# Attention and a fast-matrix-product SwiGLU block on one core: fewer and larger transfers, reciprocals between two transposes, one layout for all queries and keys

## The chip, the core and the metric

The kernel runs on one core of one Trainium2 chip. The core has a matrix engine (PE, TensorE) with its weight loader (PEld), a vector engine (DVE), a scalar engine (ACT), a general engine (POOL, GpSimd) and a queue engine (SP) that issues transfers. Each engine takes its instructions strictly in the order in which they were emitted, and a transfer that SP or ACT issues is carried out by 16 DMA engines that all queues share. The metric is the device time of one execution in microseconds (us); lower is better.

## The reference

An attention block with normalised queries and keys feeds a SwiGLU block. Shapes: 8 batches, 12 heads, 448 positions, 64 per head; 3584 tokens of 768, hidden width 1536.

```python
def rmsnorm(x, g):
    rms = np.sqrt(np.mean(x * x, axis=-1, keepdims=True) + 1e-06)
    return x / rms * g
q_n, k_n = (rmsnorm(q, g_q), rmsnorm(k, g_k))
scores = scale * np.matmul(q_n, k_n.transpose(0, 1, 3, 2))
attn = np.exp(scores - np.max(scores, axis=-1, keepdims=True))
attn = attn / (np.sum(attn, axis=-1, keepdims=True) + 1e-09)
attn_out = np.matmul(attn, v)
...
x = attn_out.transpose(0, 2, 1, 3).reshape(B * S, H * D)
g = x @ w_gate
silu = g * (1.0 / (1.0 + np.exp(-g)))
out = silu * (x @ w_val) @ w_out
```

The three weight matrices arrive as 64-bit floats, which the kernel turns into 32-bit floats itself.

## The kernel before

**Staging.** All that runs is in `fast`. Two heads of one batch are a pair; there are 48 pairs, m = 0 to 47, six to a batch. The products with the weights use a scheme that multiplies 3x3 blocks with 15 products over two batches at a time: so there are four blocks of two batches (12 pairs) each. The order on the matrix engine is: attention of pairs 0 to 11 (`EARLY`), then for each block the up products (`up_product`, L1400: 120 units of 4 matmuls, read out by ACT and DVE) and the down products (`down_product`, L1574), and among the down products of a block the attention of the next twelve pairs.

**A pair** (`attention`, from L709) runs: load q and k (`load`, L730 to 737), on SP, and for k of pair 0 on ACT's queue; squares on ACT (L767); sums on DVE (L787 or L793); a swap of partial sums on ACT (L803); a reciprocal root on ACT and DVE (`inverse_root`, L682 to 690); scaling on POOL (L827 or L834); transposition; scores on PE (L912) into one of two PSUM buffers; exponentials on ACT (L927); weighted sums on PE (L988) with the values that L754 and L757 loaded; column sums on PE (L1019); their reciprocal on DVE (`invert`, L1054); for early pairs a product that spreads it (L1062); copy, join and division on ACT and DVE (L1077, L1080, L1084). The queries and keys of a pair take two of four buffers named `qk`; the next loads wait until the query buffer has been read by L868 (`queries`), which for the usual layout stands after DVE's block transposes (L865).

**The first two pairs** (`NATURAL`) are loaded differently: 112 partitions with four consecutive positions each, so that a row of a transfer is 1 KB; PE transposes them with an identity matrix (L853) and ACT and DVE copy the result (L859, L861). With pair 0's second square, PE also issues four products of no use to the result (L770). All other pairs are loaded with rows of 32 numbers (128 bytes), four transfers to a tensor, and DVE transposes blocks of 32 by 32.

**Weights.** 24 conversions (`convert`): 16 for the up side (four to each quarter g of the up products) and 8 for the down side. Each loads 9 blocks of 64-bit values in five transfers (L1208 three, L1210 two) to a place, lets ACT scale (L1218, L1222) and DVE round (L1240, L1246, L1252), lets POOL form 11 sums and differences of blocks (L1271, L1274), and stores 15 blocks in one transfer to a buffer in memory (L1299). `load_sides` (L1360) fetches them again for the products, in pieces of five or two block names. Places: `GT`, `HS`, `ES`, `XS`, `PAIRS`, `SPARE`, which are buffers that other work uses at other times (`PAIRS` is the pairs' `work`, `ES` holds exponentials); a load into `ES`, `PAIRS` or `GT[2]` waits for `last_exp`, the column sums of pair 11. `turns` and `counts` name the places: six conversions run beside the early pairs, eighteen afterwards, and these round by way of a PSUM bank (`by_bank`).

**The order** is not written out by hand. Each step is a piece given to `Order.add` with an engine, an assumed cost, a due time (`when`, lowered by `rank`), the pieces that it follows and the buffers that it takes. `Order.run` plans a time for each piece with those costs, greedily, and emits the pieces in planned order; `LEAD` and `PAIR` set the due times of the early pairs. So a changed cost, due time or transfer count moves instructions past each other on every engine. The plan has no effect at run time other than this order; semaphores do the waiting.

## Time and profile before

| | before |
|---|---|
| median of 3 runs (lowest to highest) | 1484.42 us (1483.13 to 1485.69) |
| the profiled execution: time, span | 1484.42 us, 1482.6 us |
| PE busy | 1435.1 us (97%), 6696 matmul instructions |
| DVE, ACT, POOL busy | 914.8, 680.7, 416.0 us |
| packets moved | 409457, of which 316804 under 512 B; 193.30 MB |

The span is the time from the first to the last recorded instruction; about 1.8 us of the execution's time lie outside it. The page gives busy times per engine, then the span in 40 slices, the transfer queues, a chain of waits followed back from the end, groups of instructions by source line, and transfers. Beside the page the trace can be asked for the instructions of a stretch in order of time: start, duration, engine, line, operation, output and input with shapes, how many were merged, and, in square brackets, how long the engine stood idle before it and what released it. "SPq" and "ACTq" are the issue of transfers. The twelve early pairs take the first 140 us, the first up products 140 to 328 us.

### The profile page before, as it was taken

Reading aid. Unit: us, or ns where it says so; the run is one execution under the profiler, and the core shown is the slowest. Engines: PE = TensorE matmul, PEld = TensorE weight load, DVE = VectorE, ACT = ScalarE, POOL = GpSimd, SP = SyncE. Lnnn points to the kernel's source line nnn. Section 1 sums busy time; section 2 is a strip of 40 time slices with the busy share of each in tenths; the row PEclk is TensorE's granted clock in tenths of the full one; section 3 lists DMA queues with packets and bytes.
Section 4 is the critical chain, followed back from the end, with each engine's and each line's share of the span. In section 5 each row is a group of like instructions: output and inputs, shape, how many; then the busy total and the mean of one; then the engine's idle time right before and its main releaser. Section 6 shows DMA issues by size and latency. Waiting matters only on the chain.

```text
span 1482.6 us, 19482 instructions
## 1 busy us (share of the span) xinstructions
PE 1435.1 (97%) x6696; PEld 680.7 (46%) x6696; DVE 914.8 (62%) x1403; ACT 680.7 (46%) x1358; POOL 416.0 (28%) x470
## 2 busy tenths in 40 slices
PE   6989999999999999999999999999999999999998
PEld 2434554443444455544444445554444445555553
DVE  3878897877978544355886733454786753432533
ACT  5864544437775321445767422354676532122100
POOL 3545585636444100012534200011343410000000
PEclk8999999999999999999999999999999999999999
DMA  6677999974453431533344432352444442222235
GB/s 166 160 162 215 294 331 335 289 213 92 98 117 84 111 107 71 144 98 89 78 110 107 101 118 72 110 132 77 97 101 103 89 123 85 80 98 73 83 98 107
DMA packets 409457, 193.30 MB, mean 130 GB/s; under 512 B 316804, under 2 KB 391428, under 8 KB 403204
## 3 DMA queue, kind: packets, MB, share of 16 engines
q1 hardware_dynamic: 397840, 190.35, 47.8%
q10 hardware_dynamic: 11380, 1.61, 0.7%
q8 instruction: 55, 0.90, 0.3%
q14 instruction: 54, 0.44, 0.1%
q0 software_dynamic: 128, 0.00, 0.0%
HBM read 157.29 MB, written 34.60 MB: 129 GB/s over the span
## 4 chain that ended last, share of the span: by engine, by line
PE 73%; ACT 3%; DVE 3%; issue 1%; DMA 1%; SPq 1%; ACTq 0%; DVEq 0%
PE mm L1574 22%; PE mm L1400 20%; PE at L1400 20%; PE st L912 6%; PE at L988 5%; PE st L1019 1%; ACT spare L1072 1%; ACT es L927 1%; SPq L737 1%; DVE rd L1054 1%; DVE ss L807 0%; DMA work<-in_k_dram 0%; DMA out_dram<-spare 0%; DVE ss L793 0%; ACT ss L803 0%
## 5 line engine op out<-in xcount | busy, mean ns | idle before, releaser
L1400 PE MATMUL at<-xs,ws 128*128 128x448 f32 x960 | 400.6, 540 | 4.3 <-DVE v L1346 3.1
L1400 PE MATMUL mm<-xs,ws 128*128 128x448 f32 x960 | 401.0, 540 | 3.6 <-DVE spare L1348 2.2
L1400 PEld LDWEIGHTS at<-xs,ws 128*128 128x128 f32 x960 | 181.9, 190 | 184.8 <-issue 172.1
L1400 PEld LDWEIGHTS mm<-xs,ws 128*128 128x128 f32 x960 | 181.6, 190 | 184.3 <-issue 172.0
L834 POOL TENSOR_TENSOR work<-work,rr 128x448 f32<-128x448 f32 x92 | 101.8, 1126 | 480.1 <-DVE rr L690 353.3
L1574 PE MATMUL mm<-gt,ws 128*128 128x448 f32 x448 | 177.2, 545 | 0.0
L912 PE MATMUL st<-work 64*64 64x448 f32 (+1 forms) x1536 | 156.4, 514 | 18.0 <-ACT es L927 7.5
L1344 DVE TENSOR_TENSOR gt<-gt,mm 128x448 f32<-128x448 f32 x64 | 39.7, 620 | 184.2 <-PE mm L1400 181.9
L1574 PE MATMUL mm<-hs,ws 128*128 128x448 f32 x384 | 152.1, 545 | 0.9 <-DVE ss L688 0.9
L927 ACT ACTIVATE es<-st 128x896 f32<-128x896 f32 x129 | 114.1, 912 | 54.3 <-PE at L988 42.6
L932 POOL TENSOR_TENSOR sums<-es 128x896 f32<-128x896 f32 x36 | 75.8, 2104 | 196.0 <-PE st L1019 83.4
L1474 ACT ACTIVATE st<-gt 128x448 f32<-128x448 f32 x96 | 52.3, 546 | 168.9 <-DVE gt L1348 90.3
L1072 ACT COPY spare<-rd 32x224 f32<-32x224 f32 x288 | 108.1, 375 | 35.4 <-DVE rd L1054 31.1
L1574 PEld LDWEIGHTS mm<-gt,ws 128*128 128x128 f32 x448 | 82.9, 190 | 84.2 <-issue 80.6
L988 PE MATMUL at<-es,v 64*64 64x448 f32 x1032 | 109.9, 544 | 2.7 <-DVE ss L688 2.5
L1342 ACT COPY gt<-mm 128x448 f32<-128x448 f32 x80 | 42.5, 532 | 140.4 <-PE mm L1400 140.4
L1574 PEld LDWEIGHTS mm<-hs,ws 128*128 128x128 f32 x384 | 71.1, 190 | 72.9 <-issue 70.6
L912 PEld LDWEIGHTS st<-work 64*64 64x64 f32 x1536 | 50.8, 135 | 98.8 <-issue 38.1
L1342 ACT COPY v<-at 128x448 f32<-128x448 f32 x96 | 51.1, 532 | 85.1 <-PE at L1400 81.0
L932 POOL TENSOR_TENSOR sums<-sums,es 128x896 f32<-128x896 f32 x36 | 78.7, 2186 | 2.8
L865 DVE STREAM_TRANSPOSE work<-work 128x448 f32<-128x448 f32 x92 | 56.6, 627 | 25.5 <-POOL work L834 22.8
L988 PEld LDWEIGHTS at<-es,v 64*64 64x64 f32 x1032 | 39.5, 134 | 63.0 <-issue 58.7
(161 smaller groups left out, 1589.1 us busy)
## 6 DMA issues: line engine op xcount, KB each, us to landing
ws<-up_sides SPq DMA_DIRECT2D x32, 1024.0 KB, 5.0
ws<-down_sides SPq DMA_DIRECT2D x16, 1024.0 KB, 5.0
ws<-down_sides SPq DMA_DIRECT2D x28, 512.0 KB, 4.3
ws<-up_sides SPq DMA_DIRECT2D x16, 768.0 KB, 4.4
work<-in_q_dram SPq DMA_DIRECT2D x184, 56.0 KB, 2.4
work<-in_k_dram SPq DMA_DIRECT2D x184, 56.0 KB, 2.4
out_dram<-spare SPq DMA_DIRECT2D x168, 56.0 KB, 1.9
v<-in_v_dram SPq DMA_DIRECT2D x96, 96.0 KB, 2.6
```

What stands on the lines that cost most here:

```text
L834: nc.gpsimd.tensor_tensor(out=tiles["t", m][:, x], in0=tiles["qk", (m, x)], in1=rr.to_broadcast([P, NC, C]), op=ALU.mult,)
L865: nc.vector.transpose(to, tiles["t", m][:, x].rearrange("p c f -> p (c f)"))
L912: nc.tensor.matmul(st[ds(D * x, D), h, 0:n], tiles["KT", m][rows, ds(P * j + D * of_keys, D)], tiles["QT", m][rows, ds(Q * of_queries, n)] ...
L927: nc.scalar.activation(e, tiles["st", (m, j)][:, :, 0 : S * width(j) // P], AF.Exp)
L932: nc.gpsimd.tensor_tensor(out=to, in0=tiles["e", (m, 0)] if j == 1 else to, in1=e, op=ALU.add)
L988: nc.tensor.matmul(tiles["at", (m, x)][ds(D * h, D), queries], tiles["v", m][rows, j, h], tiles["e", (m, j)][rows, h], start=j == 0, stop= ...
L1072: nc.scalar.copy(inv[ds(D * h + C * to, C), ts(x, Q)], tiles["rd", m][ds(D * h + C * x, C)])
L1342: nc.scalar.copy(to, ps)
L1344: nc.vector.tensor_tensor(out=to, in0=old, in1=ps, op=ALU.add)
L1400: nc.tensor.matmul(ps(), w[:, at, which, c], xs[:, SLOT[x], c], start=fresh and c == 0, stop=c == NC2 - 1, skip_group_check=True,)
L1474: nc.scalar.activation(take(*act, [P, 2, TB])[:, 0, 0:S], to, AF.Silu)
L1574: nc.tensor.matmul(banks[s][:, 0:S], w[:, at, s, g], where[x][:, g], start=fresh and g == 0, stop=g == NG - 1, skip_group_check=True,)
```

## The change

1. `NATURAL` and everything that served it are gone: the identity, L770, L853, L859, L861. Pairs 0 and 1 are loaded and transposed like all others. `LEAD` is 14.0 in place of 10.0.
2. `load_six`: for the early pairs the values of three pairs come in one step of five transfers into half of `spare`, in place of four transfers to each pair. There are two such halves, so the third step waits for the weighted sums of pair 2 and the fourth for those of pair 5.
3. `invert`: DVE transposes the sums in blocks of 32 by 32, takes the reciprocal of one column of each block (7 numbers to a partition), and transposes them back with the column repeated.
4. `convert`: raw values lie behind the converted ones; three transfers with three blocks each in place of five; the order of the blocks and of the 15 stored blocks changes with it, so that a fetch by `load_sides` is often one run in place of two.
5. The sixth early conversion uses `GT[0]` for a second time in place of `SPARE`; a load into `SPARE` waits for `last_exp` too; the early conversions have a rank of 30 in place of 0.

```diff
-    EARLY = 2 * NPAIR
-    NATURAL = (0, 1)
-    UP_SUMS = (8, 1, 7, 13, 10, 14, 3, 5, 11, 0, 4)
-    DOWN_SUMS = (1, 10, 14, 3, 11, 0, 4, 5, 8, 7, 13)
-    BLOCKS = (6, 2, 12, 9)
+    UP_SUMS = (10, 14, 3, 8, 1, 7, 13, 5, 11, 0, 4)
+    DOWN_SUMS = (3, 10, 14, 1, 11, 0, 4, 5, 8, 7, 13)
+    BLOCKS = (6, 9, 2, 12)
...
-    LEAD, PAIR = 10.0, 9.0
+    LEAD, PAIR = 14.0, 9.0
...
+        def load_six():
+            x = take("ve", m // 3, None)
+            for j in range(NJ):
+                for p in (0, D) if j == NJ - 1 else (0,):
+                    n = D if j == NJ - 1 else P
+                    rows = v[b][2 * c : 2 * c + 6, ds(P * j, n)].rearrange("h s d -> s h d")
+                    nc.sync.dma_start(x[ds(p, n), j], rows)
...
-            if m == 0 and x:
-                for _ in range(4):
-                    nc.tensor.matmul(banks[0], chosen[0:R, 0], of, start=True, stop=True)
...
         def invert():
-            nc.vector.reciprocal(take("rd", m, [P, Q]), tiles[den])
+            rd, rc = take("rd", m, [P, Q]), take("rc", m, [P, Q // C])
+            nc.vector.transpose(rd, tiles[den])
+            nc.vector.reciprocal(rc, rd.rearrange("p (c i) -> p c i", i=C)[:, :, 0])
+            every = rc.rearrange("p (c one) -> p c one", one=1).to_broadcast([P, Q // C, C])
+            nc.vector.transpose(rd, every)
...
         inv = add(
-            "DVE", 1.52, when + 4.0, invert, after=[all_sums], uses=[] if of_bank else [den],
-            takes=[("rd", m)],
+            "DVE", 0.95, when + 4.0, invert, after=[all_sums], uses=[] if of_bank else [den],
+            takes=[("rd", m), ("rc", m)],
         )
...
-        rank = 20.0 if by_bank else 0.0
+        rank = 20.0 if by_bank else 30.0
...
-        raw, dst = places[place][:, 0 : 2 * VALUES], places[place][:, 2 * VALUES : PLACE]
+        dst, raw = places[place][:, 0:VALUES], places[place][:, VALUES:PLACE]
-        wait = [last_exp[0]] if place in (ES, PAIRS, GT[2]) else []
+        wait = [last_exp[0]] if place in (ES, PAIRS, GT[2], SPARE) else []
...
-            for i, n, rows in ((0, 2, (1, 3, 0)), (2, 2, (0, 2, 2)), (5, 3, (0, 3, 1))):
-                nc.sync.dma_start(to[:, i : i + n], src(slice(*rows[:2]), rows[2]))
-            for i, k, n in ((4, 0, 0), (8, 2, 2)):
-                nc.sync.dma_start(to[:, i], src(k, n))
+            for at, n in ((slice(3, 8, 2), 0), (slice(0, 3), 1), (slice(8, 3, -2), 2)):
+                nc.sync.dma_start(to[:, at], src(slice(0, 3), n))
-            "SP", 2.5, when - 12.0, load, after=[staged.get(place), *wait], kb=1152, early=3.0
+            "SP", 1.6, when - 12.0, load, after=[staged.get(place), *wait], kb=1152, early=3.0
...
-        sides = places[place].rearrange("p (b f) -> p b f", f=P)[:, 7:22]
-        at = {x: i for i, x in enumerate(sums)}
+        sides = places[place].rearrange("p (b f) -> p b f", f=P)[:, 5:20]
+        at = {x: i for i, x in enumerate((*BLOCKS, *sums))}
...
-    turns = [(*XS, *GT[:2], HS, SPARE), (ES, PAIRS, GT[2], SPARE, HS), (ES, PAIRS, HS, SPARE), (ES, HS)]
+    turns = [(*XS, *GT[:2], HS, GT[0]), (ES, PAIRS, GT[2], SPARE, HS), (ES, PAIRS, HS, SPARE), (ES, HS)]
```

The order of the built programs shows what moved. On SP, the sixth raw load of weights stood between the keys of pair 7 and the values of pair 8; it now stands behind the last keys of the early pairs. The third step of values stands before the queries of pair 6, the fourth before those of pair 9. On DVE, the block transposes of pair 11 stand behind the reciprocal of pair 10, and the first conversion by bank that follows the early pairs is a second one in `HS`, ahead of the one in `ES`. On PE, one up product and the spread of pair 10 stand ahead of the weighted sums of pair 11. The first fetch of the second quarter's weights stood behind the raw loads into `ES` and `PAIRS`; it now stands behind the stores from `PAIRS` and from `GT[2]` and the raw load into `PAIRS`.

## The prediction

> **What bounds the kernel now.** First the page's head. PE is busy 97% of the span, so only PE's idle and slow stretches can be won.
>
> ```profile
> PE 1435.1 (97%) x6696; PEld 680.7 (46%) x6696; DVE 914.8 (62%) x1403; ACT 680.7 (46%) x1358; POOL 416.0 (28%) x470
> ...
> PEclk8999999999999999999999999999999999999999
> DMA  6677999974453431533344432352444442222235
> ```
>
> The second and third lines cut the span into 40 slices. Transfers are near full only in slices 5 to 8 (148 to 297 us), where the weights are converted. 1482.6 - 1435.1 = 47 us of idle PE; the busy times by stretch put 23.5 of them before 140 us, 10 into 140 to 420 and 14 into all the 1063 us behind, the last stores among them. So the change is decided in the early pairs and shortly behind them. Next, these stretches (us; then busy time and instructions of PE, PEld, DVE, ACT, POOL, the granted clock, the transfers' share, GB/s):
>
> ```profile
> 60.00:70.00 10.00, 10.00 (x122) 4.46 (x113) 8.58 (x15) 8.76 (x17) 5.54 (x11) 1.00 0.57 99
> 70.00:80.00 10.00, 7.42 (x84) 3.70 (x82) 7.92 (x14) 6.96 (x14) 7.67 (x12) 1.00 1.02 270
> 80.00:90.00 10.00, 6.84 (x82) 3.36 (x82) 6.99 (x9) 6.51 (x10) 3.71 (x6) 0.91 0.74 164
> 90.00:100.00 10.00, 10.00 (x96) 4.04 (x88) 5.35 (x12) 7.11 (x17) 5.68 (x10) 0.75 0.68 158
> 120.00:130.00 10.00, 8.23 (x100) 3.51 (x96) 9.83 (x13) 6.48 (x9) 7.51 (x12) 1.00 0.82 288
> ```
>
> Up to 70 us ACT and DVE pace the pairs together. From 70 to 90 all engines lose, with the transfers full at first; towards the end DVE is full. The column sums (L1019) give the pace: pair 0 ends at 37.6 us, 1 at 45.0, 5 at 82.1, 6 at 97.8, 8 at 113.1, 10 at 133.7, 11 at 139.1. One step, from pair 5 to 6, takes 15.7 us where about 9 are usual. The order in time of SP, ACT and PE says why:
>
> ```profile
> 70.32 3.58 SPq L1208 DMA_DIRECT2D spare<-in_moe_w_gate_dram  x3
> ...
> 77.50 0.55 SPq L1299 DMA_DIRECT2D up_sides<-xs  x1
> 78.37 4.86 SPq L737 DMA_DIRECT2D work<-in_q_dram  x4
> 83.28 2.21 SPq L737 DMA_DIRECT2D work<-in_k_dram  x4
> ...
> 87.86 0.58 ACT L767 ACTIVATE work<-work 128x448 f32<-128x448 f32 x1 [1.84 <-DMA work<-in_k_dram]
> 88.35 0.53 ACT L927 ACTIVATE more<-st 128x448 f32<-128x448 f32 x1
> ...
> 88.92 3.27 PE L912 MATMUL st<-work 64*64 64x448 f32 x16 [3.16 <-ACT more L927]
> ```
>
> The raw load of the sixth conversion and a store stand on SP ahead of pair 8's queries. Their issue takes 4.86 us where 1.9 to 2.0 are usual, the keys land late, ACT waits at their square, the exponentials of pair 7 stand behind that square, and PE idles 3.16 us. It then runs slow: the same 16 matmuls take 3.27 us here, 1.70 at 100.35 us. At 76.22 PE waited 2.48 us more, behind pair 7's late keys.
>
> **The change part by part.** PE needs no more instructions than before; each term says how much earlier or later PE gets through.
>
> *The first two pairs.* Removed: 8 warming matmuls (6.75 us from 6.83 us) and 16 transposes. Added: rows of 128 bytes for 1 KB, four issues of 0.48 us for one of 0.45, so +1.5 us on SP for each of three tensors, and a swap (0.88 us) and four block transposes (0.62 each) in place of two copies a pair. Following the lines in order: SP issues q0, q1, k1 until 0.75 + 3 x 1.95 = 6.6 us; ACT issues k0 by about 3.4; landing takes at most 3.7 us in this trace, so k0 is there by 7.1 and k1 by 10.3. Then square 0.58, sum 1.08, swap 0.88, 0.19, root 0.46, three times 0.2, POOL twice 0.92: 12.7 us. DVE's order puts pair 1's sum first (ready at 10.3 + 0.58 + 1.08, about 12.6 us behind ACT's other steps), then 2 x 0.62 and the queries' 0.67: first scores at 14.6 to 16.5 us. Before they start at 16.45, because PE was busy with the warming products until 12.93 and DVE was held twice. The second pair is then ahead by some 5 us, but ACT has about 3 us less of weight conversion behind it. I take -1 us, from -2 to +3. The rows that bear on the lost warming: at 16.45 and 20.26 us the scores ran at full rate (8 matmuls in 0.98 us), at 28.41 slow again (16 in 3.27). So warming bought a few microseconds at most, and the upper end of +3 holds it.
>
> The Trainium skill, "TensorE: Matmul & The Clock Gate", Part 1, says that an idle array runs at half rate until about 3.4 us of sustained work, which speaks against dropping the warming products; going by it this term would be about 1.7 us worse. "DMA: Bandwidth & Descriptors", Specifications, asks for 512 bytes or more in a transfer's run, which speaks against the new loads of the first pairs; this trace has 316804 of 409457 packets below that already.
>
> *Fewer issues on SP.* Values: a pair's four issues take 0.92 + 1.27 = 2.19 us, twelve pairs 26.3. Three pairs take 3 x 0.46 + 2 x 0.63 = 2.6, four times: 10.6. Raw weights: 1.46 + 0.96 = 2.42 to 1.46, five times before the last pair. About 20 us of SP's early time go, and the sixth raw load leaves the stretch altogether: it stands behind the last keys. With it goes what made pair 8 late. The stretch costs 2.48 + 3.16 us idle and, in the slow matmuls from 88.92 to 95.7 us (3.27 for 1.70, 1.72 for 0.93, 2.42 for 1.68), 3.1 more: 8.7 us. The price of the bundling: the third step of values waits for pair 2's weighted sums and stands before pair 6's loads, the fourth waits for pair 5 and stands before pair 9's. Each adds 2.6 us of issue and some 800 KB at the 270 GB/s of the full stretch, 3 us, ahead of those keys; PE meanwhile has one pair's weighted sums, sums and scores (2.6 + 1.9 + 1.2 + 2.6 us) to do. I take two thirds: -5.8 us; bounds -8.7 and 0.
>
> *Reciprocals.* One took 1.55 us. No row has a block transpose of PSUM; 128x448 in SBUF takes 0.62, half of it 0.31, and a DVE copy takes the same 0.62 from PSUM as one (L1084) from SBUF. The 7-column reciprocal is nearest to the 0.16 to 0.19 us of DVE's narrow steps. Together 0.8 us, upper bound 1.24 + 0.2 (transposes that cost by the instruction), so -0.1 to -0.75 each. Twelve early ones take 9 us off a DVE that is 98% busy at 120 to 130 us; PE waits for L1054 there 0.93 us, and the other pairs for 1.3 us in all. The rest of DVE's relief lies beside ACT. I take -1.5 us, from -3 to 0.
>
> *The tail.* Pair 11's transposes now stand behind pair 10's reciprocal, so after pair 10's sums come 0.8 + 1.2 + 0.67, scores and exponentials in two buffers (about 4), weighted sums 2.6, sums 1.9: 11.2 us where 139.1 - 133.7 = 5.4 were; +5.8. One up product (1.50) fills a part, and the 0.77 us that the first product waited for DVE go: +3.5. Pair 10 itself is earlier by what DVE is relieved. I take +2, from -1 to +5.
>
> *The second quarter's weights.* Before, they came with nothing to spare:
>
> ```profile
> 171.35 0.51 SPq L1299 DMA_DIRECT2D up_sides<-work  x1
> ...
> 179.95 0.80 SPq L1360 DMA_DIRECT2D ws<-up_sides  x2
> ```
>
> 171.35 + about 8 to land, 179.95 + 5.0 to land = 185.0; the first product's effective start at 140.9 plus 30 x 1.504 is 186.0. Now a conversion in `HS` stands on DVE before those in `ES` and `PAIRS` (six steps of 0.76, 4.6 us, and 6.9 on POOL), and the fetch stands behind a store that needs the POOL work of `GT[2]` (done at 179.86 before) and a raw load (1.5 to 3.6 of issue). Against that, pair 10's division and five combinations move ahead of pair 11's sums: DVE starts `ES` at 11 us after these, where it was 151.61 - 139.1 = 12.5. So POOL ends `GT[2]` at 39 us after the sums, the fetch lands at 47, and PE wants it at 44.5. I take +2; bounds 0 and +10 (all of the `HS` work in series).
>
> *Nothing.* Conversions keep their ACT, DVE and POOL instructions; a fetch in one run for two saves an issue of 0.4 us, which lies beside 15 us of products. What PE loses between 238 and 288 us (4.9 us, for DVE's reads) has the same DVE work: 0, from -3 to +3.
>
> Sum: -1 - 5.8 - 1.5 + 2 + 2 = -4.3. The profiled execution took 1484.42 us, which is the median of the runs: 1480.1 us, and with the main term's ends (0 or -8.7) 1485.9 or 1477.2.
>
> **The rivals.** *The stall only moves.* The third or fourth step of values holds pair 6's or 9's keys as the raw load held pair 8's. For it: the bytes are the same, SP waits in order, and each step of values is 3 us of transfers. Against it: SP is 20 us freer. The term is 0: 1485.9, no change that a measurement can tell; so too where ACT paces the pairs (6.95 us of its rows a pair and 2.6 a conversion) and hides all relief. *The weights of the second quarter come late.* Place: the fetch before product 31; price up to 10 us in place of 2; it decides once the `ES` conversion starts on DVE later than 12.5 us after pair 11's sums. For it: the order on DVE, POOL and SP; against it: the earlier division. 1480.1 + 8 = 1488.1, slower. *The change doesn't do what it says*: two transposes and a reciprocal cost 1.44 us: +1.3 to the sum, 1481.4.
>
> **How the numbers follow.** About 0.2%, 3 us, is what a measurement of this kernel can tell from no change. Faster 0.44 (the forecast with most of the third rival), no change 0.22 (the first rival), slower 0.34 (the second, also on top of the first: 1485.9 + 8 = 1493.9, and a first stage that is late by 3). The forecast's own range is 1475 to 1484. The range for 8 in 10 goes from 1472 (8.7, 2 and 3 us won, tail and weights together +1) to 1493.
>
> **What would show it.** Right: first scores at 14 to 17 us; no PE gap over 2 us at 70 to 95 us and keys' issues of 2 us; L1012's steps near 0.8 us together; first product at 130 to 137 us; a gap of 0 to 4 us after the thirtieth product. Wrong: a gap of over 3 us before the scores of pairs 4 to 7 with ACT waiting at a square, or PE waiting for `ws` for over 5 us.

## The result, and the profile after

Over 20 runs of each, the changed kernel takes 1488.78 us (median; 1486.26 to 1490.01) and the kernel before 1483.66 us (1481.10 to 1485.94): a ratio of 1.0032, with a 95% interval from 1.0025 to 1.0039. It is slower by about 5 us. The forecast was 1480.1 us and faster; the time lies in its wide range (1472 to 1493), near what the second rival gave (1488.1 us). That nearness is luck: the rival's number keeps a gain of 5.8 us that did not come, and lacks 11.5 us that were won later. The profiled execution took 1488.38 us with a span of 1486.6 us (before 1484.42 and 1482.6), so it gives 4.0 of the 5 us.

The head of the page, after (the first line is busy time, share and instructions of each engine; the others are tenths in 40 slices):

```profile
PE 1429.1 (96%) x6672; PEld 680.7 (46%) x6672; DVE 891.2 (60%) x1501; ACT 689.0 (46%) x1370; POOL 417.0 (28%) x468
...
PEclk9998999999999999999999999999999999999999
DMA  9757899974553613342354432252344442222235
```

PE is 6 us less busy and the span 4 us longer, so 10 us more of idle PE; DVE is relieved by 23.6 us. The transfers have moved to the front (9 and 5 tenths in the first and third slice, 6 and 7 before), and the lowest clock digit from the first slice to the fourth (111 to 149 us). The stretches shown of before, after the change (us; busy time and instructions of PE, PEld, DVE, ACT, POOL, granted clock, transfers' share, GB/s):

```profile
60.00:70.00 10.00, 6.47 (x40) 2.51 (x44) 8.56 (x16) 8.04 (x16) 5.79 (x9) 0.66 0.98 232
70.00:80.00 10.00, 9.84 (x128) 4.25 (x124) 9.06 (x18) 9.73 (x19) 5.54 (x7) 1.00 0.49 105
80.00:90.00 10.00, 8.53 (x80) 3.75 (x76) 9.83 (x17) 5.01 (x12) 9.61 (x15) 0.83 0.79 161
90.00:100.00 10.00, 9.92 (x136) 4.82 (x128) 7.25 (x14) 5.54 (x13) 1.90 (x3) 1.00 0.39 105
120.00:130.00 10.00, 8.96 (x95) 3.86 (x93) 9.62 (x14) 3.72 (x5) 7.06 (x8) 0.84 0.89 296
```

In the weak stretch at 70 to 90 us PE now idles 1.6 us, where it idled 5.7; 60 to 70, which was full, now does a third of its matmuls at a clock of 0.66. The order in time of SP, ACT and PE there:

```profile
46.38 5.50 SPq L761 DMA_DIRECT2D spare<-in_v_dram  x5
51.98 3.13 SPq L734 DMA_DIRECT2D work<-in_q_dram  x4
55.15 2.38 SPq L734 DMA_DIRECT2D work<-in_k_dram  x4
...
56.92 0.58 ACT L782 ACTIVATE work<-work 128x448 f32<-128x448 f32 x1 [1.83 <-DMA work<-in_q_dram]
...
59.59 0.58 ACT L782 ACTIVATE work<-work 128x448 f32<-128x448 f32 x1 [0.53 <-DMA work<-in_k_dram]
60.07 0.53 ACT L883 ACTIVATE more<-st 128x448 f32<-128x448 f32 x1
...
60.65 0.98 PE L868 MATMUL st<-work 64*64 64x448 f32 x8 [3.00 <-ACT more L883]
64.36 1.02 PE L868 MATMUL st<-work 64*64 64x224 f32 x8 [2.73 <-ACT work L842]
```

This is the picture that the prediction showed for pair 8, one stretch earlier: the third step of values takes 5.50 us of issue (2.6 were assumed), the queries and keys behind it land late, ACT waits at their squares (1.83 and 0.53 us), an exponential stands behind the second square, PE waits 3.00 and 2.73 us.

Where the two executions stand, by the ends of the pairs' column sums and the starts of up products (us; a product is a unit of four matmuls, and for the last one the start of its last matmul is given):

| | before | after | difference |
|---|---|---|---|
| sums of pair 0, 3, 4, 5 | 37.7, 63.5, 71.7, 82.2 | 27.1, 56.7, 74.9, 82.3 | -10.6, -6.8, +3.2, +0.1 |
| sums of pair 6, 8, 10, 11 | 97.9, 113.2, 133.7, 139.1 | 93.3, 113.0, 133.6, 148.6 | -4.6, -0.2, -0.1, +9.5 |
| product 3 of the first block | 143.9 | 150.9 | +7.0 |
| product 31 | 186.8 | 202.3 | +15.5 |
| last up product of the first block | 328.0 | 340.0 | +12.0 |
| first product of block 1, 2, 3 | 503.9, 854.2, 1204.4 | 512.4, 860.2, 1208.0 | +8.5, +6.0, +3.6 |

So the start brings nothing by pair 10; pair 11 loses 9.5 us (one product is done within, so product 3 is 7.0 us late), and product 31 loses 8.5 more than product 3; everything behind wins back: 3.5 in the rest of the first block, 3.5 in the first attention stage (last up product to the next block's first: 175.9 to 172.4), 2.5 in each of the two later ones (165.3 to 162.8). From product 31 on, PE has one gap of over 0.6 us (0.66 at 294.80) in the first block: its 90 products at 1.504 us, 135.4 us, fill nearly all of the 137.7 us up to 340.0.

Pair 11, on POOL, PE, DVE and ACT:

```profile
118.63 2.10 POOL L1229 TENSOR_TENSOR hs<-hs 128x128 f32<-128x128 f32 x3
...
123.34 2.57 POOL L823 TENSOR_TENSOR work<-work,rr 128x448 f32<-128x448 f32 x2
...
133.50 1.02 PE L1022 MATMUL mm<-rd,chosen 128*128 128x224 f32 x4
134.56 0.62 DVE L1044 TENSOR_TENSOR xs<-xs,mm 128x448 f32<-128x448 f32 x1 [1.75 <-PE mm L1022]
135.10 0.41 DVE L1011 STREAM_TRANSPOSE rd<-mm 128x224 f32<-128x224 f32 x1
135.54 0.20 DVE L1012 RECIPROCAL rc<-rd 128x7 f32<-128x7 f32 x1
135.78 0.41 DVE L1014 STREAM_TRANSPOSE rd<-rc 128x224 f32<-128x224 f32 x1
136.11 1.13 DVE L839 STREAM_TRANSPOSE work<-work 128x448 f32<-128x448 f32 x2
...
138.00 3.21 PE L868 MATMUL st<-work 64*64 64x224 f32 x24 [0.45 <-ACT work L842]
...
142.55 0.92 ACT L883 ACTIVATE es<-st 128x896 f32<-128x896 f32 x1 [0.29 <-PE st L868]
```

The scalings (L823) are done at 125.9 us, behind side sums of the weights; the transposes stand behind pair 10's reciprocal and come 10 us after that; the scores follow. So in this execution the order on DVE holds the transposes, and their inputs have long been there. The reciprocal itself is late: on DVE it stands behind the division of pair 9 (L1044), and that waits 1.75 us for the product that spreads pair 9's reciprocals (L1022), which stands on PE behind pair 10's sums. The fetch for product 31, on SP, and PE:

```profile
182.26 0.55 SPq L1257 DMA_DIRECT2D up_sides<-work  x1
189.59 0.55 SPq L1257 DMA_DIRECT2D up_sides<-gt  x1
190.24 3.59 SPq L1168 DMA_DIRECT2D work<-in_moe_w_gate_dram  x3
193.93 1.13 SPq L1317 DMA_DIRECT2D ws<-up_sides  x2
...
202.32 3.13 PE L1357 MATMUL mm<-xs,ws 128*128 128x448 f32 x4 [9.14 <-DMA ws<-up_sides]
```

The last sides that the fetch needs are stored at 182.26. The fetch is issued 11.7 us later, behind another store that waits for POOL and a raw load. The sides must have landed first; the store at 189.59 took 6.0 us to land, and if this one took as long, some 5.7 of the 11.7 us (an estimate) are the order on SP. 8.4 us after its issue PE starts, having waited 9.14, and runs its first product slow (3.13 us for 1.67).

### The profile page after: what moved, and what is told of

The parts are those of the page before. It is cut to its first block, busy times and chain, and to the rows that moved or that the text cites. A ratio compares the mean times of both kernels' runs of the same rounds, so it can differ in the third digit from the quotient of the medians.

```text
span 1486.6 us, 19408 instructions
## 1 busy us (share of the span) xinstructions
PE 1429.1 (96%) x6672; PEld 680.7 (46%) x6672; DVE 891.2 (60%) x1501; ACT 689.0 (46%) x1370; POOL 417.0 (28%) x468
## 4 chain that ended last, share of the span: by engine, by line
PE 75%; DVE 1%; ACT 1%; issue 1%; DMA 0%; ACTq 0%; DVEq 0%
PE mm L1531 23%; PE mm L1357 19%; PE at L1357 19%; PE st L868 7%; PE at L944 6%; PE st L975 1%; ACT spare L1032 1%; ACT es L883 0%; DMA out_dram<-spare 0%; DVE spare L1306 0%; DVE sums L894 0%; DVE ss L810 0%; DVE st L1204 0%; DVE es L1210 0%; ACT work L842 0%
## 5 line engine op out<-in xcount | busy, mean ns | idle before, releaser
L823 POOL TENSOR_TENSOR work<-work,rr 128x448 f32<-128x448 f32 x96 | 105.4, 1117 | 514.0 <-DVE rr L691 353.3
L868 PE MATMUL st<-work 64*64 64x448 f32 (+1 forms) x1536 | 159.5, 522 | 27.7 <-ACT work L842 20.0
L888 POOL TENSOR_TENSOR sums<-es 128x896 f32<-128x896 f32 x36 | 75.2, 2088 | 169.1 <-PE st L975 74.9
L944 PE MATMUL at<-es,v 64*64 64x448 f32 x864 | 88.2, 537 | 0.0
L782 ACT ACTIVATE work<-work 128x448 f32<-128x448 f32 x96 | 53.9, 573 | 23.2 <-DMA work<-in_q_dram 15.9
```

The source lines that it names most:

```text
L782: nc.scalar.activation(tiles["t", m][:, x], tiles["qk", (m, x)], AF.Square)
L823: nc.gpsimd.tensor_tensor(out=tiles["t", m][:, x], in0=tiles["qk", (m, x)], in1=rr.to_broadcast([P, NC, C]), op=ALU.mult,)
L868: nc.tensor.matmul(st[ds(D * x, D), h, 0:n], tiles["KT", m][rows, ds(P * j + D * of_keys, D)], tiles["QT", m][rows, ds(Q * of_queries, n)] ...
L888: nc.gpsimd.tensor_tensor(out=to, in0=tiles["e", (m, 0)] if j == 1 else to, in1=e, op=ALU.add)
L944: nc.tensor.matmul(tiles["at", (m, x)][ds(D * h, D), queries], values(rows, j, h), tiles["e", (m, j)][rows, h], start=j == 0, stop=j == NJ ...
```

## The experiments

All runs are compared with the kernel before on the same chip; a second number is that kernel's median in those runs. "Before, with" and "after, with" name the kernel that was edited.

**The reciprocal alone, from both sides.** `b_recip`: before, with the new `invert`, planned at 1.52 us still.

```diff
-            nc.vector.reciprocal(take("rd", m, [P, Q]), tiles[den])
...
+            nc.vector.transpose(rd, tiles[den])
+            nc.vector.reciprocal(rc, rd.rearrange("p (c i) -> p c i", i=C)[:, :, 0])
...
+            nc.vector.transpose(rd, every)
```

> The kernel before with the new reciprocal alone (transpose, reciprocal of 7 columns, transpose), its planned 1.52 us kept, so that the order of every engine is that of before. Theory: the two later attention stages were each about 2.4 us faster in the changed kernel, and DVE's 0.5 us a pair is what they gained; with about 1 us in the first stage this run is 4 to 6 us faster than before, 1478 to 1480 us. Rival 1 (DVE's relief lies beside ACT and PE, the later stages gained by another part of the change): 1483 to 1484 us. Rival 2 (three short steps leave DVE's readers late): slower than 1485 us.

1482.44 us (1484.39), ratio 0.9986 [0.9977, 0.9995]. The first attention stage takes 176.0 us (175.9 before), the later ones 164.8 each (165.3). So the instruction alone is worth 2 us (0.7 to 3.4), half of what the theory said and close to the forecast's term.

`a_oldrecip`: after, with the old reciprocal, planned at 0.95 us still.

> The changed kernel with the old reciprocal of 128x224 put back, its planned 0.95 us kept, so that the order of every engine is that of the changed kernel. Theory: what the new reciprocal is worth shows from the other side, so 4 to 6 us slower than the changed kernel, 1493 to 1495 us, with the first products of the third and fourth block of up products about 2.4 us later against each stage's start. Rival: 1488 to 1490 us, the later stages keep their time.

1493.58 us, ratio 1.0064 [1.0050, 1.0077], against 1.0032 for the changed kernel: 4.7 us. The first attention stage takes 2.5 us more (174.9), the later ones 0.9 (163.7). In the changed order the instruction is worth about twice as much (the intervals of the two gains overlap), and the traces put most of the difference into the first attention stage; and a later stage is 1.6 us shorter than before even with the old instruction, so that part does not come from the instruction (`b_recip95`, below, shows that it comes from the order).

**The second quarter's weights.** `a_wait`: after, with the raw load for the second conversion in `HS` held until the last column sums, so that `ES` and `PAIRS` go first.

```diff
-        wait = [last_exp[0]] if place in (ES, PAIRS, GT[2], SPARE) else []
+        wait = [last_exp[0]] if place in (ES, PAIRS, GT[2], SPARE) or by_bank else []
```

> The changed kernel, with every raw load of the second and later groups of conversions held until pair 11's column sums (before this the load into hs was not), so that the ES and PAIRS conversions come ahead of the HS one on DVE and POOL; the order up to pair 11's sums is unchanged. Theory: the missing 6.9 us of POOL work ahead of ES and PAIRS is what made PE wait 9.1 us at product 31; the wait falls below 2 us and the time to 1479 to 1482 us. Rival (the chain of conversions as a whole paces the first block, and HS, now behind, is late for the third quarter): the wait moves to product 61 or to the first down products, 1485 to 1489 us.

1501.92 us, ratio 1.0121 [1.0105, 1.0136]. The theory fell, and the time is above the rival's too. The order did change, yet SP and PE, in this run:

```profile
181.03 0.56 SPq L1257 DMA_DIRECT2D up_sides<-work  x1
189.02 0.56 SPq L1257 DMA_DIRECT2D up_sides<-gt  x1
190.00 3.27 SPq L1168 DMA_DIRECT2D work<-in_moe_w_gate_dram  x3
193.37 1.16 SPq L1317 DMA_DIRECT2D ws<-up_sides  x2
...
201.53 3.19 PE L1357 MATMUL mm<-xs,ws 128*128 128x448 f32 x4 [9.05 <-DMA ws<-up_sides]
```

With `HS` out of the way the sides come only 1.2 us earlier: DVE now waits 3.94 us for ACT's scaling of the raw values of `ES`, which can't be loaded before the last sums. The `HS` conversion that the prediction put in the way lay in time that was idle anyway. The first attention stage then grows to 183.1 us.

`a_first`: after, with the first block's fetches ranked up on SP.

```diff
-                early=8.0,
+                early=8.0, rank=60.0 * (n == 0),
```

> The changed kernel, with the fetches of the first block's up weights ranked ahead of other work on SP: the second quarter's fetch now stands behind the store of GT[2]'s sides but ahead of the raw load into work, and later fetches move ahead of stores in the same way. Theory: of PE's 9.1 us wait at product 31 the raw load's 3.6 us go, so product 31 starts at 198 to 200 us; since all four variants run so far end the first block of up products at 340 to 342 us wherever it began (142 to 151 us), little of it reaches the end: 1486 to 1489 us. Rival: the gap is the whole loss and 3 to 4 us come out at the end as well, 1484 to 1485 us.

1495.38 us (1483.95), ratio 1.0075 [1.0062, 1.0088]. Product 31 starts at 199.3 us, as expected for the raw load's share, and PE waits 5.75 us. The block still ends at 339.6, and the first attention stage takes 180.3 us (172.4), with PE waiting 2.69, 1.55 and 1.74 us in it, so the time is above what theory and rival gave; why the moved fetches make that stage longer is not shown.

**Pair 11's scalings.** `a_scale`: after, with these ranked above the side sums on POOL.

```diff
-            add(
+            order.add(
                 "POOL", 1.0, ready - 9.0, lambda x=x: scale(x), after=[rr], port=True,
+                rank=90.0 if m == EARLY - 1 else rank,
```

> The changed kernel with pair 11's two scalings ranked above the side sums of weights on POOL, so that they don't stand behind the sums of HS. Theory: pair 11's step of 15.0 us (5.4 before) comes from these scalings, done at 125.9 us, and from the transposes that the order then puts behind pair 10's reciprocal; the step falls to 8 to 11 us, everything behind moves with it, and the time falls by 4 to 6 us to 1483 to 1485 us. Rival (the conversion in gt, 8.9 us on DVE and POOL, sets the end of the stage either way): the first full product stays at 142 to 149 us and the time at 1487 to 1489 us.

1493.24 us (1484.39), ratio 1.0053 [1.0040, 1.0067]. DVE's transposes of pair 11 now stand at 129.93 us, ahead of pair 10's reciprocal, and the step falls to 9.6 us (sums at 143.2), as expected. PE then stops elsewhere:

```profile
136.43 7.61 SPq L1169 DMA_DIRECT2D es<-in_moe_w_val_dram  x3
...
152.85 1.40 SPq L1258 DMA_DIRECT2D up_sides<-gt  x1
...
163.09 3.36 PE L1358 MATMUL mm<-xs,ws 128*128 128x448 f32 x4 [12.90 <-ACT gt L1301]
```

Results of the first products are copied into `gt`, where the sixth conversion's sides must have been stored first. POOL had them at 135.2, but here the store stands on SP behind four raw loads, the first of which waits for pair 11's sums.

`a_scale_store`: the same, with those raw loads made to follow that store.

```diff
-        wait = [last_exp[0]] if place in (ES, PAIRS, GT[2], SPARE) else []
+        wait = [last_exp[0], staged.get(GT[0])] if place in (ES, PAIRS, GT[2], SPARE) else []
```

> The changed kernel with pair 11's scalings ranked above the side sums, as in a_scale, and the raw loads that wait for pair 11's column sums made to follow the store of gt's sides as well, so that SP issues this store before it waits. Theory: the wait of 12.9 us was the store's place on SP; it goes, the products run from 143 us, pair 11's shorter step (9.6 us for 15.0) is kept until product 31, where PE still waits 7 to 10 us for ws, since that fetch hangs on pair 11's sums as before: product 31 at 195 to 199 us, the first block's end at 333 to 337 us, block 1 at 506 to 510 us and the time at 1482 to 1486 us. Rival: the first block ends at 339 us or later again, held by the conversions as a whole, 1487 us or more.

1488.03 us (1484.27), ratio 1.0024 [1.0015, 1.0033]. PE and DVE in this run:

```profile
152.19 1.77 PE L1358 MATMUL mm<-xs,ws 128*128 128x448 f32 x4 [2.16 <-ACT gt L1301]
160.18 0.62 DVE L1303 TENSOR_TENSOR gt<-gt,mm 128x448 f32<-128x448 f32 x1 [5.23 <-PE mm L1358]
```

The wait of 12.90 is 2.16 us, so its cause is shown, and by the ratios 4 us come out against `a_scale`. But product 31 starts at 201.2, only 1.1 us earlier than in the changed kernel though the pairs end 5.5 us earlier: DVE stands 5.23 us before a readout of the products that the order puts ahead of the `ES` conversion. The block ends at 339.5, as the rival said.

**Values and places.** `a_vspare`: after, with one pair's values at a time and the sixth conversion in `SPARE`.

```diff
-    turns = [(*XS, *GT[:2], HS, GT[0]), (ES, PAIRS, GT[2], SPARE, HS), (ES, PAIRS, HS, SPARE), (ES, HS)]
+    turns = [(*XS, *GT[:2], HS, SPARE), (ES, PAIRS, GT[2], SPARE, HS), (ES, PAIRS, HS, SPARE), (ES, HS)]
...
-        if not early:
+        if True:
```

> The changed kernel with the values loaded for one pair at a time again and the sixth conversion back in spare, in place of gt; everything else as changed. Theory (the stall moved to the third step of values, and what it cost was taken back by pair 5): PE's gaps at 60 to 66 us (5.7 us idle, some 5 more slow) go, a similar gap appears where the sixth raw load now stands (pairs 4 to 7), the first product starts within 3 us of the changed kernel's 142.4, and the time is 1487 to 1490 us. Rival 1 (the bundle is what made the changed kernel slow): 1481 to 1484 us. Rival 2 (the bundle is worth the 5.8 us of the forecast): 1493 to 1495 us.

1491.69 us (1483.95), ratio 1.0055 [1.0043, 1.0067]. The gaps at 60 to 66 us are gone; others of 3.50 and 3.66 us stand at 32.7 and 48.0. Pair 11's sums end at 149.6, product 31 starts at 203.8. Against the changed kernel's ratio of 1.0032 the bundle, with the place that goes with it, gains some 3 us in this order: it is neither what made the kernel slow nor a gain of 5.8 us.

`b_ve`: before, with the bundled values and the sixth conversion in `gt` (a raw load into `spare` then waits for the last sums, as in the changed kernel).

> The kernel before with the values loaded for three pairs at a time and so, spare being taken, the sixth conversion in gt; nothing else. Theory: what the bundle costs is the place of the sixth conversion, since the first results of the up products go into gt and wait for its sides: pair 11's sums end no later than before (139.1), but PE then waits 8 us or more for ACT's copies into gt, product 31 starts after 195 us and the time is 1488 to 1496 us. Rival 1: the issues saved on SP are worth the 5.8 us of the forecast and the place costs nothing, 1478 to 1481 us. Rival 2: no effect, 1482 to 1486 us.

1512.21 us (1483.97), ratio 1.0191 [1.0166, 1.0216]. The pairs do run ahead, as far as the forecast's main term said and further: sums of pairs 6, 8 and 10 at 84.5, 101.9 and 125.4 against 97.9, 113.2 and 133.7. Then:

```profile
137.40 1.42 SPq L1237 DMA_DIRECT2D es<-in_moe_w_val_dram  x3
...
146.58 0.53 SPq L1328 DMA_DIRECT2D up_sides<-gt  x1
...
156.61 3.08 SPq L1328 DMA_DIRECT2D up_sides<-hs  x1
162.75 0.83 SPq L1389 DMA_DIRECT2D ws<-up_sides  x2
...
168.85 3.32 PE L1429 MATMUL mm<-xs,ws 128*128 128x448 f32 x4 [16.74 <-issue]
...
183.34 3.35 PE L1429 MATMUL mm<-xs,ws 128*128 128x448 f32 x4 [5.77 <-ACT gt L1371]
```

The weights were left behind: the stores of the first quarter's own sides (the two from `gt` that precede the one from `hs`; the first is shown) stand behind raw loads that wait for the last sums, the fetch for the first products is issued at 162.75 and lands 6.0 us later, when PE starts, and the copies into `gt` cost 5.77 us more. POOL ends the fourth conversion at 136.0 us here, at 106.8 before. The theory had the direction and the wait for `gt`; the larger wait, 16.74 us ahead of the first product, it did not have, and the time is far above its 1488 to 1496 us.

`a_vspare_scale`: `a_vspare` with pair 11's scalings ranked as above.

> The changed kernel with values for one pair at a time, the sixth conversion in spare (this alone ran 1491.7 us, pair 11's sums at 149.6 us), and pair 11's scalings ranked above the side sums on POOL. Theory: with gt free the shorter step of pair 11 is not taken back by a wait for gt, so sums at 142 to 146 us, product 31 at 196 to 200 us (203.8 without the rank) and the first block's end at 334 to 339 us (341.9). Rival: something else makes the first block end at 340 to 342 us in every variant of the changed kernel, and PE waits elsewhere for what is gained.

1503.49 us (1483.97), ratio 1.0124 [1.0108, 1.0139]. The theory fell: pair 11's step is 4.5 us, but pair 10's is 19.9 (PE waits 5.91 us for queries at 131.0); product 31 at 202.6, the block's end at 347.3.

**The first two pairs.** `b_nonat`: before, with `NATURAL` empty and no warming products.

```diff
-    NATURAL = (0, 1)
+    NATURAL = ()
-            if m == 0 and x:
+            if natural and m == 0 and x:
```

> The kernel before with its first two pairs loaded and transposed in the usual layout and without the warming products, nothing else. Theory: first scores at 14.5 us and pair 0 done at about 27 us as in the changed kernel, but the lead of 8 to 10 us is given back at a stall among pairs 3 to 8, because ACT, DVE and the transfers pace the pairs; first product within 2 us of 139.9 and the time at 1482 to 1486 us. Rival 1: half of the lead or more lasts until the first product (135 us), 1478 to 1480 us. Rival 2: the plan comes out worse, later first product, above 1487 us.

1486.82 us (1483.95), ratio 1.0021 [1.0012, 1.0030]. Pair 0 is done at 26.7 us, pair 6 at 91.0, pair 7 at 104.9 (104.8 before), pair 11 at 139.1 (139.1), the first product starts at 139.9 (139.9). A lead of 11 us is spent by pair 7. The profiled execution (1485.08 us) is among the quickest of this kernel and its up products of blocks 1 to 3 start 0.6 us later than before; where the rest of the 2.9 us lies is not shown.

**Planned costs and raw loads.** `b_recip95`: `b_recip` planned at 0.95 us. `b_mix`: the same, but only from pair 12 on. `b_late`: only from pair 24 on.

```diff
-            "DVE", 1.52, when + 4.0, invert,
+            "DVE", 0.95, when + 4.0, invert,
...
+            "DVE", 1.52 if early else 0.95, when + 4.0, invert,
...
+            "DVE", 1.52 if m < 2 * EARLY else 0.95, when + 4.0, invert,
```

The three added lines belong to `b_recip95`, `b_mix` and `b_late`, in this order.

> The kernel before with the new reciprocal planned at 0.95 us, as in the changed kernel (the run of the new reciprocal in the old order was 1482.4 us). Theory: of the 2.5 us that each later attention stage gained in the changed kernel 0.9 are the instruction's and 1.6 the order planned with the shorter cost, so the two later stages (block 1's last product to block 2's first, 165.3 us before) take 163 us each, and the time is 1478 to 1480 us. Rival 1: the stages gained by another part of the change, 164.8 us each as in the run in the old order, 1482 to 1483 us. Rival 2: the new order costs the first block what the stages gain, 1483 us or more with stages of 163 us.

1495.11 us (1483.95), ratio 1.0088 [1.0072, 1.0104]: the later stages take 162.8 us, and block 1 starts at 518.8 (505.4 with the cost left at 1.52). The same instructions, another order, 12.7 us: theory right on the stages, second rival right on the sum.

> The kernel before with the new reciprocal, planned at the old 1.52 us for the first twelve pairs and at 0.95 us for the later ones, so that the order is that of before until the first block's up products end and a new one in the three attention stages behind. Theory: planning the first twelve pairs at 0.95 us is what cost the first block (first product at 145.9 us, block 1 at 518.8), and planning the later ones at it is what the later stages gain: block 1's first product at 502 to 506 us, the two later stages 163 us each (165.3 before), 1477 to 1480 us, faster than both kernels. Rival: the later stages take 164.8 us, as with the instruction alone, 1482 us.

1481.70 us (1483.97), ratio 0.9979 [0.9969, 0.9988]; block 1 at 506.3, later stages 162.8 us each. Theory right on both places, but the first attention stage is 178.2 us long in this order (176.0 with `b_recip`), so the sum is 2 us short of it.

> The kernel before with the new reciprocal, planned at the old 1.52 us in the first block and the attention stage behind it, and at 0.95 us in the two later stages. Theory: gains and losses are separate, so the first block and its stage are those of the run with the instruction alone (block 1 at 504 to 506 us) and the two later stages take 162.8 us each: 1478 to 1480 us, faster than both kernels by 0.3 to 0.4%. Rival: the later stages gain only if the stage before is planned so too: 1481 to 1483 us.

1478.09 us (1484.34), ratio 0.9960 [0.9948, 0.9971]: block 1 at 502.0, later stages 162.8 and 163.4 us. The time is the theory's: `b_recip` less twice 2.0 us gives 1478.4 (that block 1 starts 3 us earlier than in `b_recip` lies within what the start varies by, see the last section). It is the fastest of all, by 6 us against before and about 11 against the changed kernel.

`b_mix_raw`: `b_mix` with the raw weights in three transfers and the changed layout of the blocks, planned at 2.5 us still.

> The last kernel with the raw weights in three transfers each and the blocks and sums laid out as in the changed kernel, planned at the old 2.5 us of SP, so that the order is the same. Theory: SP issues 1 us less for each raw load, ahead of keys that were late (pair 8's), so pair 6's step of 15.7 us shortens by 1 to 2 us, half of which is lost again by the first product: 0 to 1.5 us faster than the last kernel. Rival 1 (the forecast's main term, 5.8 us for the issues, holds at least for the raw loads' share of 5 in 20 us): 1.5 to 3 us faster. Rival 2 (a load's rows land later when they are spread over three transfers): slower than the last kernel by 1 us or more.

1484.06 us (1483.97), ratio 0.9992 [0.9983, 1.0001]. Its interval overlaps that of `b_mix`; it shows no gain, and a new wait of 1.10 us for `ws` at product 31. The saved issues are not worth the forecast's share.

**The rank.** `b_rank30`: before, with the conversions of the early pairs ranked 30.

```diff
-        rank = 20.0 if by_bank else 0.0
+        rank = 20.0 if by_bank else 30.0
```

> The kernel before with the conversions of the first block ranked 30 in place of 0, as in the changed kernel, nothing else. Theory: this rank alone puts the side sums on POOL ahead of pair 11's scalings and the conversions ahead of pairs 8 to 11, and it alone makes both losses: pair 11's step grows from 5.4 to 13 us or more, PE waits 6 us or more for ws at product 31, the first block ends at 336 to 345 us and the time is 1492 to 1502 us. Rival: the tail came with the bundled values, the sixth conversion in gt or the reciprocal's planned cost, and this run stays within 3 us of before, 1481 to 1487 us.

1505.22 us (1484.34), ratio 1.0137 [1.0122, 1.0151]. POOL, SP and PE in this run:

```profile
123.72 1.11 POOL L1271 TENSOR_TENSOR hs<-hs 128x256 f32<-128x256 f32 x1
124.91 0.71 POOL L1274 TENSOR_TENSOR hs<-hs 128x128 f32<-128x128 f32 x1
125.58 2.22 POOL L834 TENSOR_TENSOR work<-work,rr 128x448 f32<-128x448 f32 x2
...
199.32 0.51 SPq L1299 DMA_DIRECT2D up_sides<-gt  x1
199.88 3.54 SPq L1208 DMA_DIRECT2D work<-in_moe_w_gate_dram  x3
203.46 1.15 SPq L1210 DMA_DIRECT2D work<-in_moe_w_gate_dram  x2
204.72 0.84 SPq L1360 DMA_DIRECT2D ws<-up_sides  x2
...
211.27 3.32 PE L1400 MATMUL mm<-xs,ws 128*128 128x448 f32 x4 [8.94 <-DMA ws<-up_sides]
```

One number brings both losses of the changed kernel: the scalings of pair 11 behind the side sums of `HS` and its transposes behind pair 10's reciprocal, at 145.24 us (pair 11's step is 15.6 us), the fetch behind the store from `gt` and a raw load, and a wait of 8.94 us where there was none. It brings a third that the changed kernel does not have: PE waits 6.40 us within pair 10, for a step of DVE.

`a_rank20`: after, with the rank at 20.

> The changed kernel with the conversions of the first block ranked 20 in place of 30, so that pair 11's scalings are due before the side sums on POOL. Theory (the rank trades pair 11 against the weights, and both are needed by the products): pair 11's step falls to 7 to 10 us and its sums to 136 to 142 us, but the sides in gt come later and PE waits for ACT's copies into gt as in the run with the scalings ranked alone; first block's end at 338 to 343 us, 1488 to 1494 us. Rival: the rank was simply too high, the first block ends at 330 to 335 us and the time is 1479 to 1484 us.

1497.98 us (1484.34), ratio 1.0093 [1.0078, 1.0107]. Pair 11's sums end at 138.0 us, but its step is 12.2, and PE waits 16.44 us for a copy into `gt`; the block ends at 342.2. The mechanism is the theory's, its price was higher: the first attention stage takes 179.9 us, 7.4 more than in the changed kernel. No run takes the rank back to 0 there.

`a_mix`: after, with the new reciprocal planned at 1.52 us for the first twelve pairs.

> The changed kernel with the new reciprocal planned at the old 1.52 us for the first twelve pairs, 0.95 us for the later ones. Theory: the order of pairs 4 to 8 changes (the planned cost moves conversions between pairs) but pair 11 and the second quarter stay as they are, since the rank sets them: step of pair 11 over 12 us, wait at product 31 over 6 us, 1486 to 1491 us. Rival: the planned cost is what spoils the first block here as it did in the kernel before (1495.1 against 1482.4 us), so 1476 to 1482 us.

1493.43 us (1484.34), ratio 1.0066 [1.0054, 1.0078]. The wait at product 31 is 8.94 us, as the theory said, and the time is 2 us above its range; the step of pair 11 is 9.7 us and that of pair 10 13.9, so it moved by one pair. The planned cost is not what spoils this kernel's first block.

## Why the prediction was wrong

The gains stood in the pairs and did not last: the first three terms put the kernel some 7 us ahead by pair 10, and it was 0.1 us ahead. The losses behind were 4 us in the sum and 15.5 us in the run, and 11.5 us came back later that the sum did not have. Of the signs of being wrong that the prediction named, the wait of over 5 us for `ws` came (9.14), and a gap before the scores that follow pair 3 came at its limit (3.00 us).

*First two pairs (-1).* The steps held: first scores at 14.77 us, within the 14.6 to 16.5 given. The sum did not: by `b_nonat` the term is +0.2%, about 3 us, the upper end. The lead was 10.6 us at pair 0, and pairs 3 to 7 spend all of it. The warming was misread: at 16.45 us before, the scores did not run at full rate. These 16 matmuls took 2.52 us at a granted clock of 0.50, and 1.36 us in `b_mix` at 1.00; only at 20.26 us they were fast (and the last warming product ended at 13.58 us; the 12.93 of the prediction is its start). After the change, the first 32 matmuls of scores take 5.51 us, 32 of the same shapes in one group later 3.38 (in `b_mix`); the granted clock reads 1.00 there, so the slow rate is read from the durations alone. The Trainium skill, "TensorE: Matmul & The Clock Gate", Part 1, says that an array that was idle runs at half rate at first; these durations agree in direction, with 2.1 us for this place.

*Fewer issues on SP (-5.8).* This step failed, and twice. The stall did move to the third step of values, as the first rival had it: the step's issue took 5.50 us, not 2.6, and pair 4's sums came 18.2 us after pair 3's. And where the stall does go, in `b_ve`, the pairs gain 8 to 13 us and the kernel loses 28. The sum priced what PE waits for in the pairs, and not what the pairs' waits were used for: DVE, ACT and POOL do the six conversions in them. In `b_ve` the pairs run ahead and the fourth conversion ends 29 us later; the stores of its sides and the order on SP then hold the first product.

*Reciprocals (-1.5).* The three steps take 1.02 us, not 0.8; alone they are worth 2 us (`b_recip`), inside the range. What was missed is the plan's part: planned at 0.95 us, the two later stages are 2.5 us shorter each, in three different kernels (162.8 us), and the first block 13 us longer in the kernel before.

*The tail (+2, at most +5).* Mis-sized: product 3 was 7.0 us later than before. The transposes behind pair 10's reciprocal were read from the order, rightly. But the sums came 15.0 us after pair 10's, not 11.2: the reciprocal started 1.5 us after pair 10's sums and not at once, behind the division of pair 9, for which the sum has no term; from the first scores to the end of the last exponentials it took 5.5 us, not about 4; the rest is 0.3 us of the reciprocal's steps and the product that stands within. Pair 10 was not earlier either, for which 1.5 us had been taken off. `a_scale` shows that the place of the transposes makes the step long.

*The second quarter's weights (+2, at most +10).* Mis-sized: product 31 loses 8.5 us more than product 3. Counted from pair 11's sums, DVE starts `ES` at 11.0 us and PE comes to wait at 44.6, both about as written, so the second rival's own condition (later than 12.5) was not met, and `a_wait` shows that the `HS` conversion does not matter. The fetch was to land at 47, and PE started at 53.7. Of these 6.7 us, 2.0 are POOL, which ended `GT[2]` at 41.0 and not 39; 1.3 are the store and the raw load on SP, 4.3 us up to the fetch's issue at 45.3, where the sum leaves 3; 3.4 are the fetch, 8.4 us from issue to PE's start, where 5.0 had been taken (before, it took 6.6 to 6.9 to land). `a_first` shows the raw load's share: 3.0 us.

*Nothing (0).* The waits for DVE's readouts before (2.09, 1.16, 0.66 and 1.02 us) shrink to one of 0.66; the block wins 3.5 us of what it lost. That is about the term's lower end, and it fits with products that run later against the conversions rather than with less work; no run separates the two.

The forecast's five terms sum to -4.3. By product 31 the changed kernel was at +15.5, and what lies behind, where the forecast counted almost nothing, gave 11.5 back. Of the causes, `b_rank30` shows that the rank alone, in the kernel before, makes both the tail and the late fetch; the prediction priced it only through the order that it read. That the rank is the cause in the changed kernel is likely but not shown: lowering it to 20 brought other waits, and 0 was not run; neither was `LEAD` changed by itself. Open is why product 31 starts no earlier than 199.3 us, and the first block ends no earlier than 339.5 us, in any of the nine variants of the changed kernel, wherever its products begin (138.8 to 151.4 us): each shows another in-order wait, on SP, DVE or ACT, and no single one was shown to hold all.

## What to carry to other kernels

Where a planner writes the order, a rank or an assumed cost is an edit of its own and can outweigh the instructions that it stands beside: run the new instruction with the old planned cost first, then let the plan change one stage at a time (here: 1482.4, 1495.1 and 1478.1 us with the same instructions). Before a stall is priced as a gain, look which work uses the idle time of the other engines, and price that work at the end. In a queue that takes its instructions in order, list what stands between the last producer's store and the fetch; that list, with durations, is the delay.

## What the runs showed of the hardware

A block transpose of 128x224 from PSUM to SBUF takes 0.41 us on DVE, and as much within SBUF with a column repeated as its input; 128x448 in SBUF takes 0.59 to 0.65, so it does not shrink in proportion. A reciprocal of 7 columns takes 0.20 us, of 224 columns 1.54.

The start varies by itself: with one order of the early pairs (before, `b_recip`, `b_mix`, `b_mix_raw`, `b_late`), pair 0's sums ended at 37.7, 38.7, 36.9, 39.0 and 35.9 us in five executions, and product 31 came at 186.8, 188.1, 186.8, 186.8 and 183.7. So differences of 2 to 4 us between single profiles of that order in the first block say nothing. The changed order repeats better: pair 10's sums ended at 133.6, 132.8, 133.9 and 132.9 us in four executions (after, `a_wait`, `a_first`, `a_oldrecip`). The later stages of one order repeat to 0.1 us (165.3 and 165.3 before, 162.8 and 162.8 after).
